# Layer A's key sums with the exponentials of four heads as PE weights and the values moving, under a newly searched order, choice of engines and buffers

## The chip, the cores and the metric

The kernel runs on 1 core of one Trainium2 chip. The metric is the device time of that core in microseconds. Before the change it is 319.97 us, the median of 3 runs (319.53 to 320.44).

## What is computed

Two attention layers, A and B, are applied in turn to one sequence of 2048 positions with 512 features: A, B, A, B, each on a layer-normalized copy of x and each added to x. There are H = 32 heads of Dh = 16. Layer A is linear attention with a softmax feature map of q and of k, layer B attends to 8 positions at distance 2 each.

```python
def _A_ref(x, wqkv, w_phi, wo):
    ...
    pq = jnp.einsum("bhsd,hdf->bhsf", q, w_phi)
    pk = jnp.einsum("bhsd,hdf->bhsf", k, w_phi)
    phi_q = jnp.concatenate([_softmax(pq, axis=-1), _softmax(-pq, axis=-1)], axis=-1)
    phi_k = jnp.concatenate([_softmax(pk, axis=-1), _softmax(-pk, axis=-1)], axis=-1)
    kv = jnp.einsum("bhsf,bhsd->bhfd", phi_k, v)
    z  = jnp.einsum("bhsf->bhf", phi_k)
    num = jnp.einsum("bhqf,bhfd->bhqd", phi_q, kv)
    den = jnp.einsum("bhqf,bhf->bhq", phi_q, z)[..., None] + 1e-6
    o = num / den
    ...
x = A_x
x = x + _A_ref(_layernorm(x, axis=-1), A_wqkv, A_w_phi, A_wo)
x = x + _B_ref(_layernorm(x, axis=-1), B_wqkv, B_wo)
x = x + _A_ref(_layernorm(x, axis=-1), A_wqkv, A_w_phi, A_wo)
x = x + _B_ref(_layernorm(x, axis=-1), B_wqkv, B_wo)
```

"Key sums" are kv and z: for each head 32 rows (16 features of each sign) by 16 value columns and one column of ones, summed over all 2048 positions.

## The kernel before

The sequence is cut into 4 blocks b of 512 positions, each of 4 tiles t of 128. For each of the two A layers (L = 0, 1) there are these stages:

- a1 (`s_a1`), for each block: `mk` makes the keys of a tile with 4 matmuls (w_phi is folded into the weights `WA` at the start), `ek` takes exp(k) and exp(-k) out of PSUM on ACT into the tile `Ek`. `mv` makes the values, `ev` copies them to the tile `vaug` beside a column of ones. `t8`, `t4`, `t2`, `t1` sum the 16 features on DVE, `rr` takes the reciprocal on ACT, `mul` scales `Ek` in place. `kv` adds one tile's key sums into a PSUM bank that is held from the first tile of the layer to the last.
- a2 (`s_a2`): queries `mq`, their exponentials `eq` (two of 128x512 for each `mq`, on ACT), their sums `ms` and reciprocals `rs`.
- akv (`s_akv`): takes the finished key sums out of PSUM and makes of them `ZM` (masked z, weights of `md`) and `R` (masked kv, weights of `mo`).
- a3, a4: `md` gives denominators, `dr`, `ln`, `rho`, `bc` and `mulp` (or a trip through DRAM for some blocks) scale the queries' exponentials, `mo` multiplies by R, `ev` copies out, and `s_out` multiplies by wo, adds the residual (on DVE, or on PE with an identity matmul and an ACT copy) and normalizes for the next layer.

In `kv` before, the values of 2 heads' slices with their ones (33 columns of `vaug`) are the weights and 64 columns of `Ek` are moving, 16 matmuls for a tile, each in one half of the columns of the array:

```python
nc.tensor.matmul(out, lhsT=T["va"][:, t, q, :], rhs=T["E"][:, t, :, q * H:(q + 1) * H],
```

One 128x512 matmul of zeros (L700) starts the bank. What comes out has the features along the free axis, so akv copies the bank to `kvT` (`ev`), transposes it with 4 PE transposes (`tr`, L783), and masks it from PSUM (`z` twice, L792, and `r`, L796).

Layer B (b1, b2, b3) makes Q, K and V with `WB`, forms products on DVE (`prod`, 128x4096 each, 4 for a block), sums them on PE (`lgt`), takes exponentials, multiplies by gathered values on DVE (`pav`, 128x4096 each, 4 for a block), sums on PE (`mo`) and projects. The last block of the last layer has a form of its own (e1 to e4) on PE.

The order of all steps is written out by hand in a table, `_ORDER`: each step belongs to a thread, and a program replays the table, so each engine's queue is the table's order cut to that engine. `_CHOICE` says for each step that may run on DVE or ACT (`flex`) which it is ("1" is DVE, for `res` it is PE and ACT). `_SLOTS` gives each tile its buffer: "med" and "big" are SBUF buffers, "ps" the 8 PSUM banks.

Of the kernel before, what the change touches and what calls it, by code (L numbers as in the profile page):

```python
# [16 lines left out]
P = 128  # L17
# [16 lines left out]
VCH = NB * 8 * DV  # L34
EST = (1, 3)
# [29 lines left out]
1f 39 ch 22 2f 2d 2g 1g 29 1f 2d 1j 2f 2d 7 1h 29 1i 1k 3a 29 2n 29 2i 2n 3c 2o 2o 2o 2k 2o 2k 2q 1l cd 2h 2n
2a 2k 2f 2n 2k 3a 2o 2j 24 2q 2r 2q 2o 2o 2o 29 2y 28 2y 2y 3c 2l 2z 2v 2z 2s 2z 2z 2k 2y 2z 39 36 31 2z 36 2z
3a 3b 36 36 2v 31 2v 37 2v 31 2t 36 2z 36 2b 2b 2b 2b 2m 2m ci 36 36 2m 3a 2w 2m 2v 33 34 32 31 3c 35 2q 3c 36
3b 2x g 2x 2u 2x 30 37 2x 36 38 38 38 38 3i 3c 3h 3c 39 3b 3a 3j 3k 3k 3k 3c 3d 3c 3e 3l 3b 3m 3d 3e 5h 3n 3m
3c 3e 3e 3l 5i 3m 3q 3m 3m 4f 3m 3d 3l 5j 3e 3e 3m 5i 3m 3m 3v 3d 3e 3e bd 5h 5m 5n 5i 5i 5i 3m 3d 3e 7c 5h 7d
5p 5i 5i 5i 5r 3f 3g 3g 5i 3f 3g 5i 3w 3f 3z 3x 3f 3g 5s 3y 7e 40 41 3g 7d 5u 5v 7f 5t 3g 3p 41 42 41 41 44 3g  # L70
43 3g 43 5w 5x 5x 7f 45 46 43 43 47 43 7f 5y 3f 90 47 48 49 3g 4c 91 5x 41 4b 41 41 41 4a 92 5x 4d 60 91 4l 5z
61 5z 93 5z 4q 62 5z 4g 7d 4g 4g 4m 4q 63 ck 5z 7d 4r 93 4i 4l 63 66 64 67 7g 4s 7j 65 7h 7i 4h 4j 7k bo 4n 4q
# [2053 lines left out]
```

## Time and profile before

| | us |
|---|---|
| median of 3 runs | 319.97 |
| span of the profiled execution, first to last instruction | 318.1 |
| PE busy (97% of the span) | 307.7 |
| DVE busy (93%) | 295.6 |
| ACT busy (86%) | 275.0 |
| POOL busy (15%) | 47.2 |
| the 512 key-sum matmuls (L707), busy | 8.4 |

The profiled execution is told by its span; its own device time is not given beside the runs, whose median lies 1.9 us above the span. The busy times count an engine as busy while any of its instructions is under way. PE's matmuls are pipelined, so their own durations overlap; what one of them costs is read from the distance between starts, or from the chain of waits, which gives a group's share without overlap. Three engines are close to full here, so the table alone does not say which of them sets the end: that is read stage by stage.

### The profile page before, as it was taken

How to read it: one execution, taken by the hardware profiler on the slowest of the kernel's cores; microseconds unless marked ns; L12 is line 12 of the kernel's file. 1: busy time of each engine (PE TensorE's matmuls, PEld its weight loads, DVE VectorE, ACT ScalarE, POOL GpSimd, SP SyncE). 2: the span in 40 equal slices, each digit the busy share in tenths (PEclk: the TensorE clock that was granted, in tenths of full speed). 3: DMA queues.
4: the chain of work that ended last, by engine and by line, in shares of the span. 5: the costliest groups of instructions: out<-in, count | busy, mean ns of one | idle time of the engine just before them, and what ended most of it. 6: DMA issues, size and time to landing. Idle time of an engine off the chain costs nothing.

```text
span 318.1 us, 8900 instructions
## 1 busy us (share of the span) xinstructions
PE 307.7 (97%) x3578; PEld 152.9 (48%) x3578; DVE 295.6 (93%) x459; ACT 275.0 (86%) x639; POOL 47.2 (15%) x60
## 2 busy tenths in 40 slices
PE   8999999899999999999999999989999999999994
PEld 4644456445454444444444455544444544444552
DVE  6999996998999999999999999689998999999994
ACT  4999999999898778999999999899999867697751
POOL 6000000000004212000000000033141644045000
PEclk9999999999999999999999999999999999999999
DMA  7977100005794989939894600004289875565664
GB/s 203 358 186 148 36 2 4 2 19 145 165 178 100 156 141 136 144 66 140 145 134 62 69 0 2 4 19 134 59 185 137 140 133 134 105 178 126 158 152 170
DMA packets 45789, 36.37 MB, mean 114 GB/s; under 512 B 30832, under 2 KB 41136, under 8 KB 45744
## 3 DMA queue, kind: packets, MB, share of 16 engines
q1 hardware_dynamic: 45216, 35.75, 56.3%
q8 instruction: 29, 0.48, 0.7%
q14 instruction: 16, 0.13, 0.2%
q10 hardware_dynamic: 528, 0.02, 0.1%
HBM read 11.13 MB, written 3.25 MB: 45 GB/s over the span
## 4 chain that ended last, share of the span: by engine, by line
PE 87%; DVE 5%; ACT 5%; DMA 1%; issue 1%; SPq 0%; DVEq 0%; ACTq 0%
PE PS L967 23%; PE PS L553 18%; PE PS L632 9%; PE PS L644 9%; PE PS L737 6%; PE PS L1128 4%; PE PS L1066 4%; PE PS L1185 2%; DVE Eq L855 2%; PE PS L707 2%; PE PS L940 1%; PE PS L482 1%; PE PS L556 1%; PE PS L1200 1%; PE PS L1082 1%; DMA x<-in_A_x_dram 1%
## 5 line engine op out<-in xcount | busy, mean ns | idle before, releaser
L967 PE MATMUL PS<-xnT,WB 128*128 128x512 bf16 x336 | 76.8, 380 | 0.1
L1059 DVE TENSOR_TENSOR prod<-QT,K 128x4096 bf16<-128x4096 bf16 x28 | 63.4, 2287 | 0.5 <-POOL K L993 0.5
L1121 DVE TENSOR_TENSOR pav<-PT,Vg 128x4096 bf16<-128x4096 bf16 (+1 forms) x29 | 62.9, 2214 | 0.2
L967 PEld LDWEIGHTS <-WB 128*128 128x128 bf16 x336 | 37.3, 114 | 36.4 <-issue 3.3
L745 ACT ACTIVATE Eq<-PS 128x512 bf16<-128x512 f32 x64 | 36.3, 619 | 0.0
L638 ACT ACTIVATE Ek<-PS 128x512 bf16<-128x512 f32 x64 | 35.1, 622 | 0.2 <-PE PS L632 0.2
L553 PEld LDWEIGHTS <-oT 128*128 128x128 bf16 x236 | 21.9, 98 | 26.6 <-issue 1.3
L737 PE MATMUL PS<-xnT,WA 128*128 128x512 bf16 x128 | 32.0, 380 | 0.5 <-DVE s L829 0.3
L578 ACT ACTIVATE sqd<-x 128x512 bf16<-128x512 bf16 x48 | 29.9, 631 | 2.2 <-DVE x L571 2.0
L644 PE MATMUL PS<-WA,xnT 128*128 128x512 bf16 x128 | 31.6, 379 | 0.0
L632 PE MATMUL PS<-WA,xnT 128*128 128x512 bf16 x128 | 31.0, 379 | 0.2 <-ACT WA L204 0.2
L571 DVE SCALAR_TENSOR_TENSOR x<-PS,x 128x512 bf16<-128x512 f32 x46 | 30.2, 684 | 0.7 <-PE PS L553 0.7
L204 ACT CAST oT<-PS 128x512 bf16<-128x512 f32 (+1 forms) x50 | 26.7, 597 | 3.8 <-PE PS L1128 2.1
L553 PE MATMUL PS<-WoA,oT 128*128 128x512 bf16 x128 | 29.8, 380 | 0.0
L553 PE MATMUL PS<-WoB,oT 128*128 128x512 bf16 x108 | 26.5, 379 | 0.0
L204 ACT CAST K<-PS 128x512 bf16<-128x512 f32 x30 | 17.3, 593 | 3.1 <-PE PS L967 1.9
L632 PEld LDWEIGHTS <-xnT 128*128 128x128 bf16 x128 | 12.3, 98 | 15.2 <-issue 1.0
L644 PEld LDWEIGHTS <-xnT 128*128 128x128 bf16 x128 | 12.2, 98 | 14.5 <-issue 0.4
L690 DVE TENSOR_TENSOR Ek<-Ek,rk 128x4096 bf16<-128x4096 bf16 (+1 forms) x10 | 18.6, 1860 | 0.4 <-ACT rk L685 0.4
L737 PEld LDWEIGHTS <-WA 128*128 128x128 bf16 x128 | 11.6, 98 | 14.6 <-issue 1.7
L466 DVE TENSOR_SCALAR xn<-x,rstd,nmr 128x512 bf16<-128x512 bf16 x48 | 18.1, 424 | 0.6
L204 ACT CAST V<-PS 128x512 bf16<-128x512 f32 x26 | 15.2, 596 | 2.6 <-PE PS L967 2.6
(175 smaller groups left out, 505.1 us busy)
## 6 DMA issues: line engine op xcount, KB each, us to landing
Vg<-V SPq DMA_DIRECT2D x112, 131.5 KB, 4.3
Prho<-rd SPq DMA_DIRECT2D x8, 512.0 KB, 6.1
x<-in_A_x_dram SPq DMA_DIRECT2D x3, 512.0 KB, 6.6
WB<-in_B_wqkv_dram SPq DMA_DIRECT2D x3, 512.0 KB, 9.8
out_dram<-x SPq DMA_DIRECT2D x6, 256.0 KB, 2.3
wraw<-in_A_wqkv_dram SPq DMA_DIRECT2D x4, 256.0 KB, 4.5
vd<-Vs SPq DMA_DIRECT2D x2, 272.0 KB, 2.9
x<-in_A_x_dram SPq DMA_DIRECT2D x4, 128.0 KB, 3.4
```

The costliest lines, as they stand in the source:

```text
L204: self.nc.scalar.copy(out=out, in_=in_)
L553: nc.tensor.matmul(y[:], lhsT=lh(t, c), rhs=Wo()[:, c, :], start=(c == 0), stop=(c == NB - 1 and not onpe))
L571: nc.vector.scalar_tensor_tensor(out=xb[:, t, :], in0=T[t][:], scalar=1.0, in1=xb[:, t, :], op0=ALU.mult, op1=ALU.add, **kw)
L578: nc.scalar.activation(out=sqd[:], in_=xb[:, t, :], func=ACT.Square, accum_out=T["ss"][:, t:t + 1])
L632: nc.tensor.matmul(pk[:], lhsT=xnT[:, t, k, :], rhs=self.WA[:, k, D:2 * D], start=(k == 0), stop=(k == NB - 1))
L638: nc.scalar.activation(out=T["E"][:, t, s, :], in_=T["k", t][:], func=ACT.Exp, scale=1.0 - 2.0 * s)
L644: nc.tensor.matmul(pv[:], lhsT=xnT[:, t, k, :], rhs=self.WA[:, k, 2 * D:3 * D], start=(k == 0), stop=(k == NB - 1))
L737: nc.tensor.matmul(pq[:], lhsT=self.WA[:, k, hb * P:(hb + 1) * P], rhs=xnT[:, :, k, :], start=(k == 0), stop=(k == NB - 1))
L745: nc.scalar.activation(out=self.Eq[L, b][s][:, :, hb, :], in_=T[hb][:].rearrange("p (t i) -> p t i", t=4), func=ACT.Exp, scale=1.0 - 2.0 * s)
L967: nc.tensor.matmul(pp[:], lhsT=self.WB[:, k, i * D + c:(i + 1) * D:NB], rhs=xnT[:, :, k, :], start=(k == 0), stop=(k == NB - 1))
L1059: nc.vector.tensor_tensor(out=pr[:], in0=QT[:, c:c + 1, :].to_broadcast([P, NW, TB]), in1=win, op=ALU.mult)
L1121: nc.vector.tensor_tensor(out=pv, in0=PT[:, :, lo:lo + n].unsqueeze(1).to_broadcast([P, NB, 2, n]), in1=vw, op=ALU.mult)
```

## The change

In `kv`, weights and moving side change places. The weights are 128 columns of `Ek` (4 heads, both signs), the moving side is the 4 heads' 64 value columns and one column of ones. There are 8 matmuls for a tile in place of 16, into two PSUM banks in place of one, and there is no matmul of zeros. The result has the features on the partitions. Of each result only the blocks where the weights' head is the values' head are wanted. akv then needs no transposes: four copies `sh` (64 partitions x 260, two for each bank, each on ACT or DVE) put the sums into `R`, and `z` (now one) and `r` mask out of SBUF, `r` in place. `Ek` and `vaug` get layouts by groups of 4 heads; `PHI` moves from a tile of its own to a "med" buffer, and there is one "med" buffer more.

```diff
-                T["E"] = self.big([4, 2, D], "Ek")
-            nc.scalar.activation(out=T["E"][:, t, s, :], in_=T["k", t][:], func=ACT.Exp, scale=1.0 - 2.0 * s)
+                T["E"] = self.big([4, 8, 2, HQ], "Ek")
+            nc.scalar.activation(out=T["E"][:, t, :, s, :], in_=T["k", t][:].rearrange("p (g c) -> p g c", c=HQ),
+                                 func=ACT.Exp, scale=1.0 - 2.0 * s)
...
-                self.kvp[L] = self.ps()
-            K = self.kvp[L]
-            if b == 0 and t == 0:
-                nc.tensor.matmul(K[:], lhsT=self.kvT[:, 0:P], rhs=self.kvT[:], start=True, stop=True)
-            for r in range(4):
-                for h2 in range(2):
-                    for c in range(2):
-                        q = (2 * c + h2) * 4 + r
...
-                        nc.tensor.matmul(out, lhsT=T["va"][:, t, q, :], rhs=T["E"][:, t, :, q * H:(q + 1) * H],
-                                         start=(b == 0 and t == 0 and r == 0 and h2 == 0),
-                                         stop=(b == 3 and t == 3), tile_position=(0, 64 * c), skip_group_check=True)
+                self.kvp[L] = [self.ps() for _ in range(2)]
+            for g in range(8):
+                c = g // 2 * KVC
+                nc.tensor.matmul(self.kvp[L][g % 2][:, c:c + KVC], lhsT=T["E"][:, t, g, :, :],
+                                 rhs=T["va"][:, t, g, 0:KVC], start=(b == 0 and t == 0 and g < 2),
+                                 stop=(b == 3 and t == 3), skip_group_check=True)
...
-        def ev(dve):
-            self.copy(dve, self.kvT[:], self.kvp[L][:])
...
-        def tr():
-            T["t"] = pt = self.ps(BF16)
-            for g in range(4):
-                nc.tensor.transpose(pt[:, g * P:(g + 1) * P], self.kvT[:, g * P:(g + 1) * P], self.ident[:])
...
+        def sh(half, s, dve):
+            self.copy(dve, R[HQ * half:HQ * half + HQ, s, :, 0:KVC],
+                      self.kvp[L][half][HQ * s:HQ * s + HQ, 0:NB * KVC].rearrange("p (b c) -> p b c", c=KVC))
...
+            nc.vector.tensor_tensor(out=dst, in0=R[:, :, :, HQ:KVC].to_broadcast([P, 2, NB, 8]), in1=msk, op=ALU.mult)
...
         def r():
+            v = R[:, :, :, 0:HQ].rearrange("p s b (j d) -> p (s b) j d", d=DH)
+            nc.vector.tensor_tensor(out=v, in0=v, op=ALU.mult,
+                                    in1=self.mask4[:].unsqueeze(1).unsqueeze(3).to_broadcast([P, 8, 4, DH]))
...
-                                         lhsT=self.R[32 * r:32 * r + 32, self.reg(s, hb), :],
+                                         lhsT=self.R[32 * r:32 * r + 32, s, hb, 32 * (r % 2):32 * (r % 2) + 32],
...
 _ORDER = """
-8 2 i 2e 3s e3 ce 2p 23 i a 5l i i 9 i i i 5o i i i i 4e e7 1m i 0 3u 3r 0 f i e c j b 2 k 3 4 j o 5q 1m l 3 m
+8 2 2e 2p 23 i i a d i i 9 i i i i i i i 4g 1m i 0 0 f i e c 2 3 4 1m 3 j b k j o l m 0 i 1 1t 1n p o 1o q 1m 0
...
```

The three tables are new throughout: nearly every place after the head has another order, and 15 residuals in place of 17 use PE's identity matmul. Three places show how the queues of DVE and ACT differ.

DVE at the end of layer 1's key sums, before: `Ek` is scaled for the last time (L690), `ZM` and `R` are made out of PSUM, then the first block's denominators (`s`, `Ds`, `rho`).

```order
L202 CAST vaug<-PS 128x16x32
L690 TENSOR_TENSOR Ek<-Ek,rk 128x2048
L1402 TENSOR_TENSOR nb<-okc,sgn 128x2
L792 TENSOR_TENSOR ZM_123<-PS,maskH 128x2x2x8 x2
L796 TENSOR_TENSOR R<-PS,mask_98 128x256
L829 TENSOR_TENSOR s_3461<-PS,rS 128x256
L832 TENSOR_TENSOR Ds<-s_3461 128x128
```

The same place now.

```order
L204 CAST vaug<-PS 128x8x64
L693 TENSOR_TENSOR Ek<-Ek,rk 128x2048
L1397 TENSOR_TENSOR nok<-PS,thr 128x2
L1398 TENSOR_REDUCE nf<-nok 128x1
L204 CAST R<-PS 64x4x65 x2
L780 TENSOR_TENSOR ZM_122<-R,maskH 128x2x4x8
L784 TENSOR_TENSOR R<-R,mask_98 128x8x64
L816 TENSOR_TENSOR s_3207<-PS,rS 128x256
L819 TENSOR_TENSOR Ds<-s_3207 128x128
```

Two of the four copies `sh` stand on DVE ahead of the masks; the other two stand on ACT.

ACT at that place, before: the last values (`vaug`), the copy of the bank (`kvT`), queries' exponentials (`Eq`) and their reciprocal sums (`rS`).

```order
L204 CAST vaug<-PS 128x16x32 x2
L745 ACTIVATE Eq<-PS 128x4x128
L204 CAST kvT<-PS 128x512
L745 ACTIVATE Eq<-PS 128x4x128
L759 ACTIVATE rS<-PS 128x256
L760 ACTIVATE rS<-rS 128x256
```

And now.

```order
L687 ACTIVATE s_3024<-s_3024 128x128
L688 ACTIVATE rk<-s_3024 128x256
L741 ACTIVATE Eq<-PS 128x4x128 x4
L206 CAST R<-PS 64x4x65 x2
L755 ACTIVATE rS<-PS 128x256
L756 ACTIVATE rS<-rS 128x256
```

The one copy of 128x512 has become two of 64x260, and the exponential that stood behind it stands ahead of them.

DVE where layer 1's last normalization (`x_86`, block 3, for B) meets the first products of layer B, before.

```order
L1059 TENSOR_TENSOR prod<-QT,K 128x4096
L466 TENSOR_SCALAR xn<-x_85,rstd,nmr 128x512
L571 SCALAR_TENSOR_TENSOR x_86,sums<-PS,x_86 128x512 x4
L588 SCALAR_TENSOR_TENSOR q<-sums 128x4
L590 TENSOR_TENSOR q<-q,ss 128x4
L457 SCALAR_TENSOR_TENSOR nmr<-sums,rstd 128x4
L466 TENSOR_SCALAR xn<-x_86,rstd,nmr 128x512 x2
L1059 TENSOR_TENSOR prod<-QT,K 128x4096 x3
```

And now.

```order
L1046 TENSOR_TENSOR prod<-QT,K 128x4096 x2
L573 SCALAR_TENSOR_TENSOR x_86,sums<-PS,x_86 128x512
L468 TENSOR_SCALAR xn<-x_85,rstd,nmr 128x512
L573 SCALAR_TENSOR_TENSOR x_86,sums<-PS,x_86 128x512 x3
L204 CAST V<-PS 128x512
L590 SCALAR_TENSOR_TENSOR q<-sums 128x4
L592 TENSOR_TENSOR q<-q,ss 128x4
L204 CAST QT<-PS 128x512
L459 SCALAR_TENSOR_TENSOR nmr<-sums,rstd 128x4
L468 TENSOR_SCALAR xn<-x_86,rstd,nmr 128x512 x3
L1046 TENSOR_TENSOR prod<-QT,K 128x4096 x3
```

Two products have moved ahead of the last residuals, and a copy of V and one of QT now stand between the steps of the normalization.

More of the change, by code (lines that the diff above doesn't have):

```diff
@@ L806, in reg @@
+            nc.vector.tensor_tensor(out=v, in0=v, op=ALU.mult,
+                                    in1=self.mask4[:].unsqueeze(1).unsqueeze(3).to_broadcast([P, 8, 4, DH]))
+        for half in range(2):
+            for s in range(2):
+                self.flex(st, sh, half, s)
+        add(st, "DVE", z)
+        add(st, "DVE", r)
     @staticmethod
     def reg(s, hb):
[L808 removed]
+        return s * NB + hb
     def s_a3(self, L, b, dma):
```

155 lines of the change are left out of this document (71 added, 84 removed).

## The prediction

> **What bounds the kernel now.** I read the page's first part, then the engines' busy time stage by stage, and then the chain of waits and DVE's timeline at the places where the change works. The first part gives busy time and its share of the span by engine, the next line the end of the chain's summary.
>
> ```profile
> span 318.1 us, 8900 instructions
> PE 307.7 (97%) x3578; PEld 152.9 (48%) x3578; DVE 295.6 (93%) x459; ACT 275.0 (86%) x639; POOL 47.2 (15%) x60
> PE 87%; DVE 5%; ACT 5%; DMA 1%; issue 1%; SPq 0%; DVEq 0%; ACTq 0%
> ```
>
> The chain is PE's at 87%, but DVE is nearly as full, so the shares alone don't say what a us of either is worth. The stretches do: after each stretch stand its length, then PE, weight loads, DVE, ACT and POOL busy, PE's granted clock, the DMA share and GB/s.
>
> ```profile
> 51.20:57.50 6.30, 5.80 (x163) 3.51 (x163) 3.12 (x10) 5.86 (x15) 0.00 (x0) 1.00 0.01 3
> 67.50:99.00 31.50, 31.49 (x260) 15.88 (x245) 29.95 (x62) 28.51 (x68) 1.81 (x5) 1.00 0.59 128
> 99.00:145.00 46.00, 46.00 (x355) 21.60 (x358) 45.72 (x44) 39.49 (x97) 7.12 (x7) 1.00 0.86 136
> 145.00:194.00 49.00, 49.00 (x374) 22.27 (x367) 48.14 (x65) 48.45 (x115) 0.39 (x1) 1.00 0.61 82
> 204.00:216.00 12.00, 9.56 (x264) 5.49 (x265) 9.57 (x25) 10.68 (x24) 4.11 (x2) 1.00 0.12 35
> 270.00:282.00 12.00, 12.00 (x98) 5.48 (x96) 12.00 (x7) 8.89 (x19) 2.75 (x1) 1.00 0.54 125
> ```
>
> From 67 to 194 us PE has no gap and DVE almost none; ACT has slack (39.49 of 46) until 145, and none from 145 to 194 (48.45 of 49). The two ends of key sums (51 to 57, 204 to 216) are not saturated: there one engine waits for another. In the last part DVE is full (12.00 of 12) up to its last sums.
>
> ```profile
> 307.11 2.35 DVE L1121 TENSOR_TENSOR pav<-PT,Vg 128x2048 bf16<-128x2048 bf16 x2
> 309.38 0.69 DVE L571 SCALAR_TENSOR_TENSOR x<-PS,x 128x512 bf16<-128x512 f32 x1
> ```
>
> After the last `pav` (307.11 + 2.35 = 309.46) there are 8.6 us of projection, residuals and store, which the change leaves as they are. So four things set the time: PE's work before 204 us, the two ends of key sums, and DVE's work and waits from about 216 to 309.
>
> **The change part by part.**
>
> *Key-sum matmuls.* The present ones, from the chain (start, length, what) and from their line (min/median/max in ns):
>
> ```profile
> 44.51 1.98 PE PS L707 x128
> L707 PEld LDWEIGHTS <-vaug x512: 93/98/100, 44.4 to 203.7; 128*33 128x33 bf16 x171
> ```
>
> 1.98/128 is 15.5 ns for one, so 512 take 7.92 us. The new ones have 128-column weights and move 65 columns. The nearest row has the same weights and 64 columns, 16 of them up to the next group's start:
>
> ```profile
> 261.18 0.63 PE L1193 MATMUL PS<-xnT,WB 128*128 128x64 bf16 x16
> 261.64 1.03 PE L1200 MATMUL PS<-WB,xnT 128*128 128x512 bf16 x4
> ```
>
> (261.64 − 261.18)/16 = 28.8 ns, times 65/64 = 29.2 ns; 256 take 7.48 us, 0.44 less than before. Bounds: 15.5 ns, if only the moved columns count, as now (3.97 us, −3.95), and 98 ns, if each load stood on PE's path (25.1 us, +17.2). I take 29.2, the row with the same weights. The Trainium skill ("TensorE: Matmul & The Clock Gate", section "LDWEIGHTS (loading the stationary operand)") speaks against this change: it puts a load at the number of columns over 1.2 ns, 107 ns for 128 columns and 27.5 ns for 33. By it the new matmuls would be 256 × 107 = 27.3 us and the old ones 14.1 us, an estimate of +13 us. The trace disagrees with both figures: 28.8 ns a matmul behind a load of 128 columns, 15.5 ns behind one of 33.
>
> *Other PE work.* Two matmuls of zeros, eight transposes, and two residuals on the identity go away. The chain has the price of a zero matmul (the first row) and of 16 transposes (the third):
>
> ```profile
> 44.29 0.22 PE PS L700
> 204.59 0.40 PE PS L783 x4
> 228.50 0.89 PE PS L482 x16
> ```
>
> Zeros: 2 × 0.22 = 0.44. Transposes: 0.89/16 = 0.056, eight 0.44; the 0.40 for the four at 204.59 holds their latency, which belongs to the end of the sums below. A residual on the identity is one 512-column matmul, 0.22 like the zeros: 0.44. PE in all −0.44 − 0.44 − 0.44 − 0.44 = −1.76. About half, −0.9, lies ahead of layer 1's sums, where PE has no gap and nothing else becomes late: DVE loses some work there too (below). The rest lies where DVE sets the end, and I cost it at nothing.
>
> *The end of layer 1's sums.* The chain now is copy, transposes, masks, and DVE waits 1.99 us for it:
>
> ```profile
> 203.95 0.59 ACT kvT L204
> 205.03 0.29 DVE L792 TENSOR_TENSOR ZM<-PS,maskH 128x32 bf16<-128x32 bf16 x2 [1.99 <-PE PS L783]
> 205.23 0.41 DVE L796 TENSOR_TENSOR R<-PS,mask 128x256 bf16<-128x256 bf16 x1
> 206.12 0.42 DVE L829 TENSOR_TENSOR s<-PS,rS 128x256 f32<-128x256 f32 x1 [0.47 <-PE PS L821]
> ```
>
> From the last matmul's end (203.93) to `ZM` are 1.10 us. In place of copy and transposes come four `sh` of 64 x 260 in two pairs. No row has that shape; bounds are 0.29 (128 x 32) and 0.59 (the whole 128 x 512). I take 0.40, by the 128 x 256 rows at 0.41 and 0.42. A pair is 0.8, so `ZM` comes 0.3 earlier: −0.3, from −0.5 to +0.1. An exponential of queries now stands ahead of the two `sh` on ACT; if it is late, ACT's pair ends up to 0.6 later, and what waits is `ZM`, the sums `s` and every query matmul behind.
>
> *The end of layer 0's sums.*
>
> ```profile
> 51.25 0.69 DVE L202 CAST kvT<-PS 128x512 bf16<-128x512 f32 x1 [0.74 <-PE PS L707]
> 53.10 0.29 DVE L792 TENSOR_TENSOR ZM<-PS,maskH 128x32 bf16<-128x32 bf16 x2 [1.16 <-PE PS L783]
> 54.52 0.42 DVE L829 TENSOR_TENSOR s<-PS,rS 128x256 f32<-128x256 f32 x1 [0.79 <-ACT Eq L745]
> ```
>
> The copy runs at 51.25 and `s` starts 3.27 us behind it. Two copies of 0.4, a mask and the sums would be 2.1 to 2.2. But the last row waits for ACT's `Eq`, which is full there (5.86 of 6.30): with the copies gone from DVE's chain, the exponentials are late next. So 0 to −1.1; I take −0.5.
>
> *DVE and ACT work.* Counted from the order of both: residuals on DVE 46 to 48, normalized rows 48 to 45, casts of 128 x 512 (`oT`, `K`, `QT`, `V`, `vaug`, `kvT`) 25 to 27, copies of `xnT` 6 to 4, four `sh` (two in each layer), and `z` and `r` about as long as before. Prices are distances between starts:
>
> ```profile
> 219.91 1.29 DVE L202 CAST oT<-PS 128x512 bf16<-128x512 f32 x2
> 221.11 2.35 DVE L875 TENSOR_TENSOR Eq<-Eq,Prho 128x2048 bf16<-128x2048 bf16 x2
> 227.34 1.06 DVE L466 TENSOR_SCALAR xn<-x,rstd,nmr 128x512 bf16<-128x512 bf16 x3
> 229.43 0.69 DVE L202 COPY xnT<-PS 128x1024 bf16<-128x1024 bf16 x1 [0.42 <-PE PS L482]
> 230.04 0.68 DVE L571 SCALAR_TENSOR_TENSOR x<-PS,x 128x512 bf16<-128x512 f32 x1
> 230.64 0.08 DVE L571 DVE_READ_ACCUMULATOR x<-PS,x 128x1 f32 x1
> ```
>
> A cast is (221.11 − 219.91)/2 = 0.60, a residual 230.64 − 230.04 = 0.60, a row 0.35, `xnT` 0.61. That makes +1.2 − 1.05 + 1.2 − 1.2 + 1.6 = +1.75 us on DVE. By place in the order about −1.2 falls ahead of layer 1's sums, under PE's −0.9, and +2.9 behind; 0.8 of that is `sh`, counted in its chain, so +2.1 is left where DVE sets the end: casts of the first tiles of layer B and two residuals. A part of it stands in DVE's idle time from 204 to 216 (9.57 of 12), so the bounds are +1.2 and +2.1; I take +2.1, since most of those casts stand behind 216.
>
> ACT loses two residuals (0.593 each) and casts, and gets three rows, two `xnT` and four `sh`:
>
> ```profile
> L568 ACT ACTIVATE x<-PS 128x512 bf16<-128x512 f32 x17 | 10.0, 593 | 4.0 <-PE PS L556 3.8
> L468 ACT ACTIVATE xn<-x,nmr,rstd 128x512 bf16<-128x512 bf16 x16 | 12.9, 818 | 0.2 <-DVE nmr L457 0.2
> L204 ACT COPY xnT<-PS 128x1024 bf16<-128x1024 bf16 x3 | 3.0, 1009 | 0.3 <-PE PS L482 0.3
> ```
>
> About +2 us, nearly all before 145, where its slack of 6.5 us hides it; without that cover it would cost 2.
>
> *Waits of DVE ahead of layer B's products.*
>
> ```profile
> 246.01 0.16 DVE L590 TENSOR_TENSOR q<-q,ss 128x4 f32<-128x4 f32 x1 [0.79 <-ACT sqd L578]
> 246.77 0.16 DVE L457 SCALAR_TENSOR_TENSOR nmr<-sums,rstd 128x4 f32<-128x4 f32 x1 [0.60 <-ACT rstd L453]
> 247.62 6.69 DVE L1059 TENSOR_TENSOR prod<-QT,K 128x4096 bf16<-128x4096 bf16 x3
> 255.41 2.29 DVE L1059 TENSOR_TENSOR prod<-QT,K 128x4096 bf16<-128x4096 bf16 x1 [0.50 <-POOL K L993]
> ```
>
> The first two waits are filled now: a cast of V and one of QT stand in them, and two products are moved ahead of the last residuals, with the 0.50 wait for POOL's rows of K gone when K is earlier. At most −1.9, at least 0 (the casts end earlier than ACT's sum of squares, and the products wait for K instead). I take the whole, since that is the work that the +2.1 counts.
>
> *DMA.* The last gather of V is issued by SP from 290.51:
>
> ```profile
> 290.51 12.27 SPq L1028 DMA_DIRECT2D Vg<-V  x16
> Vg<-V SPq DMA_DIRECT2D x112, 131.5 KB, 4.3
> ```
>
> It is out at 302.8 and lands 4.3 us later, about when `pav` (307.11) wants it. With layer B's products up to a few us earlier it must be earlier as well; its buffer comes free with the `pav` before it, which moves along. I cost it at nothing; if the buffer comes free later than now, what waits is the last `pav`, up to 2 us.
>
> *The sum.* PE −0.9, layer 0's end −0.5, layer 1's end −0.3, DVE +2.1 − 1.9 = +0.2: −1.5 us. Against the span that is 316.6. The median of the runs, 319.97, is 1.9 above that span, so the time is 318.5.
>
> **The rivals.**
>
> *No change that can be told.* A measurement tells 0.3%, 0.96 us, from no change: 319.0 to 320.9. For it speaks that three engines are near full (97, 93, 86%): if layer 0's end gives nothing, and PE's −0.9 is met by ACT, which has no slack from 145 to 194, only −0.1 is left: about 319.9. Chance 0.26.
>
> *DVE's added work decides.* The mechanism: the casts on DVE ahead of the products are bought with nothing, since DVE waits for ACT's sum of squares all the same, or for V's PSUM. Then +2.1 stands alone from 216 to 309, with PE's −0.9 and layer 1's −0.3 against it: +0.9 to +1.2, 321.0. For it: DVE has no slack there (12.00 of 12). Against it: two waits of 0.79 and 0.60 are just a cast long. It decides where less than 0.3 us of the 1.9 is recovered. With a late last gather (+2) it is up to 322. Chance 0.19.
>
> *More waits go than counted.* Layer 0's end gives its whole 1.1 and DVE's added work stays at +1.2: −0.6 − 0.9 more, 317.0. For it: the idle 2.4 us of DVE from 204 to 216. Chance 0.17, beside 0.35 for the forecast itself.
>
> *The weight loads are not hidden.* With 98 ns of the L707 row for each of 256, +17.2: about 336. Against it stands the L1193 row with its 28.8 ns. Chance 0.03. By the Trainium skill's rule for loads, above, it would be +13 and 332; no run here yet shows these weights with 65 columns.
>
> **How the numbers follow.** Forecast 0.35 (318.5, its own range 317.7 to 319.0), more gain 0.17, no change 0.26, DVE's work 0.19, loads 0.03. Faster is 0.35 + 0.17 = 0.52, same 0.26, slower 0.19 + 0.03 = 0.22. The range reaches down to 316.6 (the rival with the larger gain, and 0.4 of the −3.95 that matmuls of 15.5 ns would bring) and up to 321.3, which leaves out the loads and the worst of DVE's case.
>
> **What the changed profile would show.** The kv matmuls at 29 ns apart, with loads beside them. `ZM` 0.8 us after the last kv matmul in place of 1.10, and no transposes. DVE's waits at `q` and `nmr` for block 3 gone or under 0.3 each, and DVE gap-free again up to the last `pav`, which ends near 308. PE without a gap from 67 to 194. I am wrong if kv matmuls are 50 ns or more apart; if `ZM` waits for ACT's pair over 1.1 us; if DVE's products wait for K or QT; or if ACT from 145 to 194 turns out to be what PE waits for.

## The result and the profile after

The changed kernel takes 330.37 us, the median of 4 runs (329.47 to 331.08), against 319.83 (319.53 to 320.44) for the kernel before beside it: a ratio of 1.0318, 95% interval 1.0292 to 1.0344. It is 10.5 us slower. The forecast was 318.5 us, with a range that ended at 321.3.

The page's first part after: span, busy time by engine, and the chain's shares.

```profile
span 329.0 us, 8374 instructions
PE 309.8 (94%) x3310; PEld 154.1 (47%) x3310; DVE 300.9 (91%) x461; ACT 275.3 (84%) x641; POOL 36.6 (11%) x60
ACT 32%; PE 28%; DVE 16%; DMA 9%; SPq 8%; issue 6%; DVEq 0%; ACTq 0%
```

No engine has much more to do (DVE +5.3, PE +2.1), but the chain, 87% PE before, now goes from engine to engine, with DMAs, SP's queue and issue in it. The loss is mostly waiting. The span is 10.9 us longer, and PE, which was nearly full before, is idle for 19.2 us of it in place of 10.4. The kernel before has no wait of PE over 1.0 us past its first 20 us; four longer ones now make 7.4 us: 1.29 for a `pav` (at 127 us), 2.08 for a product (260), 2.44 for the tile `Vx` (300) and 1.63 for issue (310). The same stretches as before the change, and two of the last part:

```profile
99.00:145.00 46.00, 44.71 (x299) 20.97 (x297) 43.22 (x43) 38.57 (x95) 5.00 (x7) 1.00 0.92 142
204.00:216.00 12.00, 10.33 (x254) 6.58 (x252) 10.29 (x23) 10.34 (x25) 1.30 (x1) 1.00 0.04 9
270.00:282.00 12.00, 11.89 (x86) 5.39 (x85) 11.82 (x7) 9.35 (x21) 5.22 (x2) 1.00 0.55 135
296.00:312.00 16.00, 11.67 (x387) 7.13 (x368) 12.51 (x12) 8.87 (x29) 0.00 (x0) 0.89 0.81 158
300.00:304.00 4.00, 3.80 (x152) 2.50 (x153) 1.83 (x2) 2.43 (x9) 0.00 (x0) 0.57 0.99 188
```

From 204 to 216 PE and DVE are busier than before (10.33 and 10.29 against 9.56 and 9.57). From 99 to 145 each has lost what it had not lost before (DVE 43.22 against 45.72), and from 296 PE idles 4.3 us of 16. Right behind its wait of 2.44 us PE's granted clock is 0.57 from 300 to 304; what that is, is told at the end. So the key sums are not where the time went. Counted against the kernel before by the starts of DVE's weighted sums (`pav`) and products, the delay is 1.1 us at the first `pav` of the last block of layer 0's B (117.04), 2.6 a few `pav` later (128.07), 5.2 at the first `pav` of layer 1's B (270.32 against 265.16), and 10.0 at the last one (317.10 against 307.11).

The key sums after, from the chain, from their line, and from DVE's timeline at the end of layer 0's and of layer 1's sums:

```profile
204.89 2.30 PE PS L703 x72
L703 PEld LDWEIGHTS <-Ek 128*128 128x128 bf16 x256 | 8.9, 97 | 1.4
52.12 0.87 DVE L204 CAST R<-PS 64x260 bf16<-64x260 f32 x2 [0.47 <-PE PS L703]
53.78 0.22 DVE L780 TENSOR_TENSOR ZM<-R,maskH 128x64 bf16<-128x64 bf16 x1 [0.79 <-ACT R L206]
54.81 0.42 DVE L816 TENSOR_TENSOR s<-PS,rS 128x256 f32<-128x256 f32 x1 [0.81 <-PE PS L808]
207.22 0.87 DVE L204 CAST R<-PS 64x260 bf16<-64x260 f32 x2 [0.54 <-PE PS L703]
208.19 0.22 DVE L780 TENSOR_TENSOR ZM<-R,maskH 128x64 bf16<-128x64 bf16 x1
```

One matmul is 2.30/72 = 31.9 ns, its load of 97 ns hidden. From the copies to `s` in layer 0 are 2.69 us (3.27 before), and from the last matmul (207.19) to `ZM` in layer 1 are 1.00 (1.10 before).

### The profile page after: what moved, and what is told of

It is laid out like the page before. It is cut to its first block, busy times and chain, and to the rows that moved or that the text cites. A ratio compares the mean times of both kernels' runs of the same rounds, so it can differ in the third digit from the quotient of the medians.

```text
span 329.0 us, 8374 instructions
## 1 busy us (share of the span) xinstructions
PE 309.8 (94%) x3310; PEld 154.1 (47%) x3310; DVE 300.9 (91%) x461; ACT 275.3 (84%) x641; POOL 36.6 (11%) x60
## 4 chain that ended last, share of the span: by engine, by line
ACT 32%; PE 28%; DVE 16%; DMA 9%; SPq 8%; issue 6%; DVEq 0%; ACTq 0%
PE PS L555 9%; ACT Ek L640 6%; DMA Vg<-V 5%; ACT Eq L741 4%; DMA Prho<-rd 4%; SPq L1015 4%; ACT sqd L580 3%; DVE Eq L842 3%; ACT oT L206 3%; DVE pav L1108 3%; PE PS L954 3%; PE PS L733 2%; PE PS L647 2%; PE PS L634 2%; DVE prod L1046 2%
## 5 line engine op out<-in xcount | busy, mean ns | idle before, releaser
L954 PE MATMUL PS<-xnT,WB 128*128 128x512 bf16 x336 | 78.1, 380 | 0.6 <-DVE x L573 0.6
L741 ACT ACTIVATE Eq<-PS 128x512 bf16<-128x512 f32 x64 | 35.2, 625 | 0.0
L573 DVE SCALAR_TENSOR_TENSOR x<-PS,x 128x512 bf16<-128x512 f32 x48 | 31.5, 683 | 2.6 <-PE PS L555 2.4
L647 PE MATMUL PS<-WA,xnT 128*128 128x512 bf16 x128 | 31.9, 379 | 0.0
L733 PE MATMUL PS<-xnT,WA 128*128 128x512 bf16 x128 | 31.3, 380 | 0.2 <-ACT bs L873 0.2
L555 PE MATMUL PS<-WoA,oT 128*128 128x512 bf16 x128 | 30.9, 380 | 0.1
L206 ACT CAST oT<-PS 128x512 bf16<-128x512 f32 (+1 forms) x53 | 29.0, 597 | 1.4 <-PE PS L1115 1.4
L468 DVE TENSOR_SCALAR xn<-x,rstd,nmr 128x512 bf16<-128x512 bf16 x45 | 18.9, 472 | 0.4
L206 ACT CAST QT<-PS 128x512 bf16<-128x512 f32 x24 | 13.9, 596 | 3.1 <-PE PS L954 3.1
```

Source lines behind the costliest of these rows:

```text
L206: self.nc.scalar.copy(out=out, in_=in_)
L555: nc.tensor.matmul(y[:], lhsT=lh(t, c), rhs=Wo()[:, c, :], start=(c == 0), stop=(c == NB - 1 and not onpe))
L573: nc.vector.scalar_tensor_tensor(out=xb[:, t, :], in0=T[t][:], scalar=1.0, in1=xb[:, t, :], op0=ALU.mult, op1=ALU.add, **kw)
L647: nc.tensor.matmul(pv[:], lhsT=xnT[:, t, k, :], rhs=self.WA[:, k, 2 * D:3 * D], start=(k == 0), stop=(k == NB - 1))
L733: nc.tensor.matmul(pq[:], lhsT=self.WA[:, k, hb * P:(hb + 1) * P], rhs=xnT[:, :, k, :], start=(k == 0), stop=(k == NB - 1))
L741: nc.scalar.activation(out=self.Eq[L, b][s][:, :, hb, :], in_=T[hb][:].rearrange("p (t i) -> p t i", t=4), func=ACT.Exp, scale=1.0 - 2.0 * s)
```

## The experiments

The runs asked in turn whether the sums, POOL's queue, SP's queue or DVE's order costs the time. Each ratio is against the kernel before, run beside it.

**The new sums in the old order.** The changed key sums run under the order, choice and buffers of before, with only what they need renamed; in layer 0 ACT then has two of the four `sh`.

```diff
 (ACT, layer 0, in the old order)
 L688 ACTIVATE rk<-s_757 128x256
+L206 CAST R<-PS 64x4x65 x2
 L741 ACTIVATE Eq<-PS 128x4x128
```

> The new key sums (kv, the four sh copies, z, r, layouts) under the order, engines and buffers of before; only the steps that exist in one version alone are put where their counterparts stood, and two banks are renamed so that the second key-sum bank is free. Theory 'order' (the loss comes from the new tables, not from the sums): 319 to 321 us, within 0.5% of before. Theory 'sums' (the sums themselves cost it: weight loads of 128 columns, two banks, four copies): 325 us or more, with gaps on PE around the kv matmuls.

It took 323.61, ratio 1.0112 [1.0092, 1.0131]. The rows of ACT and DVE at the end of layer 0's sums:

```profile
51.20 0.75 ACT L206 CAST R<-PS 64x260 bf16<-64x260 f32 x2 [2.03 <-PE PS L703]
56.71 0.42 DVE L816 TENSOR_TENSOR s<-PS,rS 128x256 f32<-128x256 f32 x1 [3.71 <-ACT Eq L741]
```

ACT stands 2.03 us in front of its two copies, the queries' exponentials stand behind them, and DVE waits 3.71 for those. That is a fault of placement, so the next run takes it away.

**The same, fitted.** All four `sh` of layer 0 go to DVE, and in layer 1 ACT's two stand behind the last exponential.

```diff
 (DVE, layer 0)
-L204 CAST R<-PS 64x4x65 x2
+L204 CAST R<-PS 64x4x65 x4
 (ACT, layer 1)
-L741 ACTIVATE Eq<-PS 128x4x128
+L741 ACTIVATE Eq<-PS 128x4x128 x2
 L206 CAST R<-PS 64x4x65 x2
-L741 ACTIVATE Eq<-PS 128x4x128
```

> old_order with its four-copy end fitted: in layer 0 all four sh on DVE (ACT's two had stood 2.03 us for the last key-sum matmul, with the queries' exponentials queued behind them and DVE's s 3.71 us late), in layer 1 ACT's two behind the last exponential. Theory 'placement' (old_order's +3.4 us is these copies' place in ACT's queue): 319.5 to 321 us. Theory 'sums' (the new sums cost the rest whatever their place): 323 us or more.

320.37 (12 runs), ratio 1.0003 [0.9993, 1.0013]: the new key sums alone are worth nothing either way, and the 10.5 us come with the new tables.

**The old sums under the new tables.** The converse.

```diff
-                nc.tensor.matmul(self.kvp[L][g % 2][:, c:c + KVC], lhsT=T["E"][:, t, g, :, :],
+                        nc.tensor.matmul(out, lhsT=T["va"][:, t, q, :], rhs=T["E"][:, t, :, q * H:(q + 1) * H],
```

> The reverse: the key sums of before (33-column weights, one bank, transposes) under the new order, engines and buffers. Theory 'order': 329 to 332 us, as the changed kernel. Theory 'sums': 318 to 322 us.

335.21, ratio 1.0461 [1.0434, 1.0487]. The tables were made for the new sums: DVE's `ZM` waits 4.7 us for the transposes here, against 3.15 in the kernel before, so the 335 has a misfit of its own in it and only agrees with the run above.

**POOL's memset.** In the changed kernel the clearing of `Qbd` stands on POOL behind a copy of K's rows that waits for ACT. POOL's and DVE's rows there (after), then the memset's row before the change:

```profile
247.66 1.55 POOL L980 COPY K<-K 128x64 bf16<-128x64 bf16 x1 [30.30 <-ACT K L206]
249.32 3.51 POOL L1149 MEMSET Qbd<- 128x4096 bf16 x1
249.64 3.34 DVE L468 TENSOR_SCALAR xn<-x,rstd,nmr 128x512 bf16<-128x512 bf16 x1
257.53 6.69 DVE L1046 TENSOR_TENSOR prod<-QT,K 128x4096 bf16<-128x4096 bf16 x3
```

```profile
229.71 3.51 POOL L1162 MEMSET Qbd<- 128x4096 bf16 x1
```

A normalized row `xn`, 0.41 long when alone (below), takes 3.34 here and ends at 252.98, with the memset (252.83). Two runs move one or the other away. The first puts this memset, and the one of `WA` behind it, where POOL is idle:

```diff
 (POOL)
 L1156 MEMSET WA 128x3072
+L1149 MEMSET Qbd 128x4096
+L1156 MEMSET WA 128x3072
 L980 COPY K<-K 128x4x16
 L996 COPY vh<-V 128x64
-L1149 MEMSET Qbd 128x4096
 L992 COPY V<-vh 128x4x16
-L1156 MEMSET WA 128x3072
```

> The changed kernel with POOL's first Qbd memset (3.5 us) and its second WA memset (2.7 us) moved ahead of the copy of K's rows, behind the first WA memset, so that they run near 217 to 224 us in place of 249 to 256. Theory 'port' (the xn on DVE that took 3.34 us in place of 0.4 waited for POOL's memset): that xn takes 0.4 us, products start 2.5 to 3 us earlier, 327 to 328.5 us. Theory 'not on the path' (other waits take its place): 330 us, with xn at 0.4 us all the same. Theory 'xn is slow for another reason': xn stays at 3.3 us and the time at 330.4.

The second gives that one row to ACT.

```diff
-L573 SCALAR_TENSOR_TENSOR x_86,sums<-PS,x_86 128x512
-L468 TENSOR_SCALAR xn<-x_85,rstd,nmr 128x512
-L573 SCALAR_TENSOR_TENSOR x_86,sums<-PS,x_86 128x512 x3
+L573 SCALAR_TENSOR_TENSOR x_86,sums<-PS,x_86 128x512 x4
```

> The changed kernel with this one xn (of block 2 of layer 1) made by ACT in place of DVE; the memsets stay where they are. Theory 'port': DVE no longer stands 2.9 us, and as ACT waits there anyway, 327 to 328.5 us, like memset_early. Theory 'not on the path': 330 us.

326.97 (ratio 1.0215 [1.019, 1.024]) and 328.61 (1.0273 [1.0247, 1.03]). DVE's rows with the early memset, then POOL's and DVE's with the row on ACT:

```profile
249.39 0.41 DVE L468 TENSOR_SCALAR xn<-x,rstd,nmr 128x512 bf16<-128x512 bf16 x1
254.36 6.69 DVE L1046 TENSOR_TENSOR prod<-QT,K 128x4096 bf16<-128x4096 bf16 x3
```

```profile
252.62 2.65 POOL L1156 MEMSET WA<- 128x3072 bf16 x1
252.99 3.08 DVE L468 TENSOR_SCALAR xn<-x,rstd,nmr 128x512 bf16<-128x512 bf16 x3
```

With the memsets away the products start 3.2 us earlier and the whole is 3.4 shorter. With the row away the next memset meets the next three rows (3.08 for 1.06), and half the gain is lost. The collision is worth 3.4 us: shown.

**SP's queue at the end of layer 0.** A transposing DMA of SP lasts 4.39 us in the changed kernel (1.93 before) and holds 24 gathers of V behind it. Two runs with the early memset move it, behind four more gathers or ahead of four.

```diff
 (SP: the first run; the second has x8 and x28)
-L1015 DMA Vg<-V 32x2104 x12
+L1015 DMA Vg<-V 32x2104 x16
 L475 DMA_TRANSPOSE xnT<-xn 128x16x128
-L1015 DMA Vg<-V 32x2104 x24
+L1015 DMA Vg<-V 32x2104 x20
```

> memset_early (326.97) with four gathers of V, whose data were ready, issued by SP ahead of the transposing DMA at 113.85 us in place of behind it. Theory 'queue' (a transposing DMA on SP waits for gathers in flight, and holds the gathers behind it, so pav stood 1.31 us at 125 us): that pav no longer waits, 325.5 to 326 us. Theory 'bandwidth' (the gathers are late because the DMA engines are busy at 0.9): the wait stays within 0.3 us, 327 us.

> memset_early, and SP issues its second-last transposition at the end of layer 0 behind 8 gathers of V in place of 12; the 4 gathers taken from ahead of it are issued behind it. Theory A (the transposition waits for the gathers in flight and holds those behind it; that is the 2.7 us at the end of layer 0): it lasts 1.9 to 2.5 us in place of 4.37 and ends near 116, the last gathers of the block come no later, the first weighted sums of layer 0's end start up to 1 us earlier, time 326.97 to 325.5. Rival B (the gathers are bound by SP's issue, 0.6 us each, and by their landing): the transposition is short, but SP waits for the normalized rows until 113.6 with four gathers unissued, those are 2.5 us later, the weighted sums wait for them, time 327 to 329.

Both lose against the early memset alone (326.97): 330.01 (1.0308 [1.0287, 1.0329]) and 329.82 (1.0327 [1.0283, 1.0372]). The size of the second loss is uncertain: its six runs lie between 327.98 and 332.59, and the longer ones have the lower mean clock of PE (0.993 at 327.98, twice; 0.989 at 329.28; 0.985 at 332.59). The trace is of a run at 327.98, 0.8 above the traced run with the early memset (327.17). SP's row of the transposition before, after, with 16 gathers ahead and with 8, and DVE's wait after and with 8:

```profile
113.11 1.93 SPq L473 DMA_TRANSPOSE xnT<-xn  x1
```

```profile
113.85 4.39 SPq L475 DMA_TRANSPOSE xnT<-xn  x1
125.08 2.29 DVE L1108 TENSOR_TENSOR pav<-PT,Vg 128x4096 bf16<-128x4096 bf16 x1 [1.31 <-DMA Vg<-V]
```

```profile
115.59 5.94 SPq L475 DMA_TRANSPOSE xnT<-xn  x1
```

```profile
113.02 1.56 SPq L475 DMA_TRANSPOSE xnT<-xn  x1
125.65 2.29 DVE L1108 TENSOR_TENSOR pav<-PT,Vg 128x4096 bf16<-128x4096 bf16 x1 [2.13 <-DMA Vg<-V]
```

The transposition is the longer, the closer gathers stand ahead of it: SP was done with issuing them 4.6, 2.6, 1.0 and 5.2 us earlier, in the order of these rows, and a gather lands 4.3 us (before) to 4.8 us (after) behind its issue. So that half of theory A is shown. But with 8 ahead the four taken away are late themselves, and `pav` waits 2.13 instead of 1.31: rival B. With 16 ahead `pav` no longer waits for gathers, but PE waits 2.70 for `xnT`, and a later `pav` 3.73 for PE. Neither place is better than the one it has.

**Later transfers on ACT's queue.** Three runs with the early memset: the four reads of `Vx` issued by ACT (first diff line), that with the 16 gathers ahead, and the 16 copies of `Qs` into `Qbd` issued by ACT (second).

```diff
-            nc.sync.dma_start(out=dst, in_=src)
+            (nc.scalar if r * 9 + j0 >= 11 else nc.sync).dma_start(out=dst, in_=src)
...
-            nc.sync.dma_start(out=self.Qbd[i][lo:lo + DH, :, g % 4, :]
+            nc.scalar.dma_start(out=self.Qbd[i][lo:lo + DH, :, g % 4, :]
```

> memset_early (326.97) with the four reads into Vx issued by ACT's queue in place of SP's, where they stood behind 26 others issued one by one (0.5 to 0.7 us each). Theory 'queue': they land about 4 us earlier, PE's wait of 2.4 us at L1323 and DVE's 2.1 us at oB go, 324 to 325.5 us. Theory 'bandwidth': the reads take longer in flight, 326.5 to 327 us.

> memset_early, gather_first and vx_act together. If the three waits are independent and on the path: the gains add, 322.5 to 324.5 us; if they share one slack: about the better of the two, 325 us.

> memset_early (326.97) with the 16 copies Qs to Qbd issued by ACT's queue in place of SP's. In memset_early SP issues DMAs from 264.98 to 306.78 us nearly without a gap, 0.5 to 0.65 us each, and begins 6.6 us later than SP before (258.38). Theory 'issue' (SP's issuing, late by the new order, sets Vx and the last gathers): SP is done with the reads into Vx 6 us or more earlier, PE's wait of 2.4 us and DVE's of 2.1 us go, 322 to 325 us. Theory 'PE and ACT' (what reads Vx is late itself): PE waits at L1323 for something else, 326 to 327 us.

They were tried because of these rows of the last part, first before the change (SP), then after (SP, PE):

```profile
258.38 2.02 SPq L1240 DMA_DIRECT2D Qbd<-Qs  x3
288.56 1.84 SPq L1257 DMA_DIRECT2D Vx<-vd  x4
```

```profile
268.19 3.00 SPq L1227 DMA_DIRECT2D Qbd<-Qs  x3
296.25 1.85 SPq L1244 DMA_DIRECT2D Vx<-vd  x4
300.20 0.20 PE L1323 MATMUL PS<-Vx,et 128*32 128x68 bf16 x1 [2.44 <-DMA Vx<-vd]
310.17 0.20 PE L1323 MATMUL PS<-Vx,et 128*8 128x68 bf16 x1 [1.63 <-issue]
```

SP begins the copies 9.8 us later than before and the reads of `Vx` 7.7 later; each costs it 0.7 to 1.0 us (2.02/3, 3.00/3). The reads on ACT gave 327.43 (1.0224 [1.0203, 1.0245]), no gain: PE's wait for `Vx` went, but `WA` was waited for 1.6 and PE's wait for issue grew from 1.6 to 2.8. All three gave 330.24 (1.0303 [1.028, 1.0326]), which is the 16 gathers' loss. The copies on ACT gave 325.25 (1.0177 [1.0147, 1.0207]): 1.7 less than the early memset alone, with intervals that overlap. Three of its four runs have a mean clock of 1.000 and lie at 325.1 to 325.4; the fourth, at 0.995, took 327.46. SP now begins the reads of `Vx` at 288.46, as early as the kernel before, and PE has no wait for them. Yet from the first `pav` of layer 1's B to the last one pass 44.6 us, against 46.5 with the early memset alone and 41.95 before: with SP on time, and ACT paying for the issue, 1.8 of these 4.5 us come back.

The same copies on ACT in the fitted old order, and together with the shorter transposition:

> old_order_fit (320.37) with the 16 copies issued by ACT's queue, as a control: in the old order nothing but 1.3 us of PE waited for these DMAs. Theory 'issue': SP is free earlier here too, but DVE's sums set the end, so 319.5 to 320.5 us.

> gather_later with the 16 copies of Qs issued by ACT (qs_act). If the end of layer 0 and SP's late queue in layer 1 are separate losses, the two gains add up: 325.25 less what gather_later gives, 324 to 325 by theory A. If PE sets the last part in any case, the time is that of qs_act, 325.2, whatever layer 0's end does. By rival B of gather_later 325 to 327.

326.03 (1.0179 [1.0153, 1.0206]), 5.7 worse than 320.37, and 327.97 (1.0253 [1.0234, 1.0271]), 2.7 worse than 325.25 and above all that was expected of it. In the first, a wait of ACT shows why; columns are the total, the times and the longest:

```profile
ACT QT L206 <- DMA Qbd<-Qs: 3.5, 1, 3.5
```

ACT's own work queues behind the copies that it issues: a `QT` waits 3.5 us while ACT issues four of them. So these copies help only where SP is late already. In the second, PE waits 2.70 us at layer 0's end, as it does without the copies, and its clock behind that wait differs; here are four us behind it, without the copies and with them:

```profile
129.00:133.00 4.00, 4.00 (x20) 1.94 (x19) 4.00 (x2) 2.98 (x7) 0.00 (x0) 1.00 1.09 151
129.00:133.00 4.00, 4.00 (x16) 1.58 (x13) 3.94 (x2) 2.15 (x4) 0.00 (x0) 0.61 1.08 152
```

So the 2.7 hold a stretch at a lower clock, and the two losses cannot be added up from these runs.

**Products ahead of the normalization.** This is half of the edit on which the forecast's −1.9 stood, made alone: in the fitted old order one product, or two, move ahead of layer 1's last normalization. They stand behind the last residuals here, where the changed kernel has them ahead, and the casts of V and QT stay where they were. The third run also gives the first product of the next block a buffer that is free; the fourth makes both edits of the third in the kernel before.

```diff
 (DVE; the second run moves x2 and leaves one of the three)
 L573 SCALAR_TENSOR_TENSOR x_86,sums<-PS,x_86 128x512 x4
+L1046 TENSOR_TENSOR prod<-QT,K 128x4096
 L590 SCALAR_TENSOR_TENSOR q<-sums 128x4
 L592 TENSOR_TENSOR q<-q,ss 128x4
 L459 SCALAR_TENSOR_TENSOR nmr<-sums,rstd 128x4
 L468 TENSOR_SCALAR xn<-x_86,rstd,nmr 128x512 x2
-L1046 TENSOR_TENSOR prod<-QT,K 128x4096 x3
+L1046 TENSOR_TENSOR prod<-QT,K 128x4096 x2
 (third run: "big" buffers, the row with the first products of layer 1)
-...2615352306...
+...3615253206...
```

> old_order_fit (320.37) with one product of layer B moved ahead of the last normalization's q on DVE, into the two waits of 0.80 and 0.60 us that the prediction counted as recoverable. Theory 'DVE sets the end there' (the prediction's step): both waits go, and with 0.5 us for POOL's rows of K 319.0 to 319.6 us. Theory 'late next': xn of the last block comes 0.9 us later, with it the transposing DMA and the gathers of V behind it on SP's queue, and the time is 320 to 321 us, with a new wait of DVE for K, QT or Vg.

> The same with two products ahead, as the changed kernel has it, so that xn of the last block comes about 3.2 us later. Theory 'DVE sets the end there': as with one product, 319.0 to 319.6 us. Theory 'late next': 321 to 324 us, the two transposing DMAs and the gathers 2 to 3 us later, and DVE or PE waits for them.

> fill (320.41) with the first product of the next block in a buffer that is free since layer 1's key sums, in place of the one that PE's L1053 had still to read (DVE stood 2.01 us for that in fill); three later tiles exchange the same two buffers. Theory 'buffer' (fill's gain turned into that wait): the wait goes, 318.5 to 319.3 us, 0.2 to 0.4% faster than before. Theory 'PE sets the end there' (the products are early and what reads them is not): 320 to 320.5 us, with the wait at a later product or at the sums of V.

> The same two edits (one product ahead of the last q, the buffer) on the kernel before, with the old key sums. If the gain is the order's and not the sums': the same time as fill_slot within 0.3%, 318.5 to 319.3 us under 'buffer', 320 us under 'PE sets the end there'.

One: 320.41, 1.0027 [1.0015, 1.0039]. Two: 324.7, 1.0149 [1.0134, 1.0164]. One with the other buffer: 320.8, 1.0023 [1.0013, 1.0034]. In the kernel before: 320.99, 1.0035 [1.002, 1.005]. None gains, and two cost 4.3 us. DVE's rows with one, then DVE's and SP's with two:

```profile
248.14 0.16 DVE L459 SCALAR_TENSOR_TENSOR nmr<-sums,rstd 128x4 f32<-128x4 f32 x1 [0.60 <-ACT rstd L455]
256.08 4.49 DVE L1046 TENSOR_TENSOR prod<-QT,K 128x4096 bf16<-128x4096 bf16 x2 [2.01 <-PE PS L1053]
```

```profile
250.57 0.16 DVE L459 SCALAR_TENSOR_TENSOR nmr<-sums,rstd 128x4 f32<-128x4 f32 x1 [0.60 <-ACT rstd L455]
252.72 2.29 DVE L1046 TENSOR_TENSOR prod<-QT,K 128x4096 bf16<-128x4096 bf16 x1 [1.22 <-ACT K L206]
260.14 4.49 DVE L1046 TENSOR_TENSOR prod<-QT,K 128x4096 bf16<-128x4096 bf16 x2 [2.56 <-PE PS L1053]
253.42 3.68 SPq L475 DMA_TRANSPOSE xnT<-xn  x2
```

With one, the wait at `q` is gone, and DVE waits 2.01 later, for PE to read a product's buffer: what is gained goes into the next wait. With a free buffer the products run up to 1.5 us earlier, and by the first `pav` 0.41 of it is left: DVE waited 0.39 for ACT's `QT` and 0.54 for PE, so DVE alone does not set the end there. With two, `nmr` comes at 250.57 instead of 246.86, the transpositions at 253.42 instead of 249.72, and K, PE's sums and the next products are late behind them (waits of 1.22 and 2.56). PE has nothing to do for 2.75 us up to 251.55, and the next stretch runs at a lower clock (1.00 with one product):

```profile
252.00:256.00 4.00, 4.00 (x12) 1.54 (x11) 2.29 (x1) 2.95 (x6) 2.36 (x1) 0.57 0.42 97
```

**One of the two put back.** With the early memset, and then with the copies on ACT as well:

```diff
-L1046 TENSOR_TENSOR prod<-QT,K 128x4096 x2
+L1046 TENSOR_TENSOR prod<-QT,K 128x4096
 L573 SCALAR_TENSOR_TENSOR x_86,sums<-PS,x_86 128x512
...
-L1046 TENSOR_TENSOR prod<-QT,K 128x4096 x3
+L1046 TENSOR_TENSOR prod<-QT,K 128x4096 x4
```

> memset_early with one of the two products that stand ahead of layer 1's last normalization put back behind it, as before had it. Theory 'late next' (the two products ahead delay xn, the transposing DMAs and the gathers, as fill_two showed in the old order with 4.3 us): normalization and transposes 1 to 2 us earlier, 325 to 326 us. Theory 'DVE sets the end': DVE waits for PE's projection instead, 327 to 328.5 us.

> one_back and qs_act together. If both act on the one late chain of SP: 321 to 324 us; if neither is on the path: 327 us.

326.75 (1.0196 [1.0158, 1.0235]) and 326.27 (1.0194 [1.0168, 1.0221]): no difference that these intervals tell. In the first, `nmr` comes 1.5 us earlier than with the early memset alone (251.66 against 253.18), but the first `pav` only 0.07 (267.04 against 267.11), and DVE waits 4.2 us in six waits for PE's projection at L573, against 2.1 in three. So rows that are 1.5 us earlier bring nothing in the new tables.

## Why the prediction was wrong, step by step

**Key-sum matmuls: right.** 31.9 ns each against 29.2 forecast; 256 are 8.2 us against 7.92 + 0.44 before with the zeros. The rival with loads on PE's path (336) is out. The Trainium skill ("TensorE: Matmul & The Clock Gate", section "LDWEIGHTS (loading the stationary operand)") would put a load of 128 columns at 107 ns and one of 33 columns at 27.5 ns, estimates by its rule. The trace's loads take 97 ns and, before, 98: near the first figure, far from the second. The prediction set these figures against the distance between matmuls, which is another thing: 31.9 ns, so that a load's length is not what a matmul costs here.

**PE's other work, −0.9; the ends, −0.5 and −0.3: nearly right in the trace, worth nothing in the time.** Layer 0's end became 0.58 shorter, with ACT's `R` late next (0.79); layer 1's `ZM` came 0.10 earlier rather than 0.3, since a copy takes 0.43 and its first waits 0.54. The fitted run has the matmuls, the zeros and the transposes of the change and equals the kernel before, to within 0.13%. Work saved at places where PE is full was counted as time saved; the run gave none of it.

**Waits of DVE ahead of layer B's products, −1.9 "taken whole": the step that failed.** The waits did go, as forecast: after the change neither `q` (255.59) nor `nmr` (256.35) waits. Without the collision DVE's own queue even gains by it. With the early memset DVE is 1.8 us late at layer 1's first product (241.50 against 239.67) and 1.2 at the seventh, whose row is here (259.95 before):

```profile
261.17 4.49 DVE L1046 TENSOR_TENSOR prod<-QT,K 128x4096 bf16<-128x4096 bf16 x2
```

What failed is the step from DVE's waits to the kernel's time: the prediction had DVE set the end from 216 to 309, so that a us of DVE's wait is a us of time. From the first `pav` of layer 1's B to the last one the kernel with the early memset takes 46.5 us against 41.95, and there PE waits 2.4 for `Vx` and 1.6 for issue, and DVE waits for ACT and PE.

The filler also has a price that the term left out: it stands ahead of what the next layer waits for. `nmr` came at 246.77 before and comes at 253.18 with the early memset, 6.4 later, since two products (4.48) and two casts (1.3) stand ahead of it for two waits of 0.79 and 0.60. The bounds said "at least 0"; in the old order the two products alone measured +4.3, and there PE waits 2.75 for what hangs on the late rows. In the new tables that price is not shown: with the early memset PE has no wait over 0.8 us between 128 and 294, and the run with `nmr` 1.5 earlier gained nothing. The order that the prediction quoted showed what stands ahead of `nmr`; it was to be followed along the path of the normalized rows as well.

Layer 0 shows the same reading at the block ahead of its last one. DVE's rows and SP's next transposition, before:

```profile
96.68 0.96 DVE L466 TENSOR_SCALAR xn<-x,rstd,nmr 128x512 bf16<-128x512 bf16 x2
97.70 1.80 SPq L473 DMA_TRANSPOSE xnT<-xn  x1
```

And after:

```profile
96.71 2.28 DVE L1046 TENSOR_TENSOR prod<-QT,K 128x4096 bf16<-128x4096 bf16 x1
99.58 0.73 DVE L468 TENSOR_SCALAR xn<-x,rstd,nmr 128x512 bf16<-128x512 bf16 x2
101.23 1.82 SPq L475 DMA_TRANSPOSE xnT<-xn  x1
```

A product stands where the rows stood, the rows are 2.9 later and the transposition 3.5, and the gathers behind it are late when the next transposition comes. That this product is the cause was not tried.

**POOL's queue: not in the sum at all.** The memset that moved behind a waiting copy cost 3.4 us, shown by its removal. The prediction read the queues of PE, DVE and ACT, not POOL's. The Trainium skill ("SBUF — State Buffer", section "Who interferes with whom") says that DVE and GpSimd share one pair of ports as an exclusive lock, which `tensor_scalar`, `copy` and `cast` can take. The trace agrees: `xn` took 3.34 us in place of 0.41 beside a memset of 3.51.

**DMA, "at nothing; up to 2 us": mis-sized.** The last gathers weren't the trouble: SP as a whole was late by 5.6 us behind the last transpositions (gathers at 259.75, 254.11 before), and by 8 to 10 for `Qbd` and `Vx`, and PE then waits for `Vx`.

**The rivals.** "DVE's added work decides" had the right sign, but put its worst at 322 and its cause, the casts on DVE, was not what cost the time. "No change" is what the new sums alone give.

**What stays open.** Of 10.5 us, 3.4 are shown to be the memset's, and the sums' share is none. The remaining 7 are only located, by the trace with the early memset: DVE is 1.8 us late at layer 1's first product, what is left of the 2.6 at layer 0's end, and loses 4.5 between the first and the last `pav` of layer 1's B. The copies on ACT give back at most 1.7. About 1.7 of the 4.5 may be PE's clock, an estimate (half of 3.4 us, below). That late normalized rows are the common cause fits the +4.3 of the old order, but the one run that made them earlier in the new tables, by 1.5 us, speaks against it. PE's issue waits of 1.4 to 2.9 us at L1323 (none over 0.5 before) have no cause that a run shows. No version here beats the kernel before.

The section on the change speaks of one "med" buffer more: it is one allocation more, and the buffers are 16 in both kernels.

## What to carry to other kernels

A wait of an engine is time of the kernel only where that engine sets the end; and a filler that is longer than the wait delays what stands behind it: follow that result to its next consumer, and price the delay there. When a reordered kernel is judged, read every queue, the idle engines' and the DMA issuers' first: a memset nobody waits for can lock a busy engine out. And put a change of arithmetic into the old order, fitted, before a new order is searched for it: here that told that it was worth nothing.

## What the runs showed of the hardware

**DVE and POOL.** Not every pair of the two collides. A memset beside `pav`, which reads two tiles in SBUF, slows neither (after: 2.23 us for a `pav` in both rows, 3.51 for the memset), while a small copy of POOL that reads SBUF stretches from 0.24 to 5.46 us beside the products (before):

```profile
274.88 3.51 POOL L1149 MEMSET Qbd<- 128x4096 bf16 x1 [10.55 <-DVE pav L1108]
270.32 6.69 DVE L1108 TENSOR_TENSOR pav<-PT,Vg 128x4096 bf16<-128x4096 bf16 x3
277.71 8.94 DVE L1108 TENSOR_TENSOR pav<-PT,Vg 128x4096 bf16<-128x4096 bf16 x4
```

```profile
248.95 5.46 POOL L993 COPY K<-K 128x64 bf16<-128x64 bf16 x1 [9.07 <-ACT K L204]
255.04 0.24 POOL L993 COPY K<-K 128x64 bf16<-128x64 bf16 x1 [0.64 <-DVE K L202]
```

**Queues.** A transposing DMA on SP's queue took 1.56, 1.93, 4.39 and 5.94 us, the longer the later the gathers ahead of it were issued. Four transfers issued by ACT held up ACT's own work for 3.5 us.

**PE's clock.** A long wait of PE costs more than its length, since the granted clock often falls to half behind it. In the changed kernel it is 0.50 from 301 to 303, behind the wait of 2.44, and the fall lasts about 3.4 us. In the traces of the twenty kernels here, from 20 us on, PE waits 18 times for 2.3 us or longer (up to 2.87), and behind 13 of these its clock is 0.50 for about as long; behind none of the 22 waits of 1.2 to 2.23 us is it. Apart from that it falls only behind the last matmuls. One such stretch takes about 1.7 us from PE (half of 3.4, an estimate), half a per cent of the span. That may be why the mean clock and the time of two runs of one kernel differ together: 325.1 to 325.4 us at 1.000 and 327.46 at 0.995 with the copies on ACT. Why it does not fall behind the other five of the 18 is not shown.
